# First batch of a fused attention and feed-forward kernel: K and Q loaded as fp32 half sequences and turned by TensorE, with one ordered queue behind them

## The chip, the cores and the metric

One core of a Trainium2 chip runs the kernel. It has TensorE for matmuls (PE in the rows; PEld is its weight load), VectorE (DVE), ScalarE (ACT), GpSimd (POOL) and SyncE (SP). DMAs are started from SP, ACT or POOL. The metric is device microseconds of one execution; lower is better.

## The reference

Attention with two kinds of heads, then a maxout feed-forward network over the concatenated heads. Shapes: B=4, H=8, S=768, D=64; 3072 tokens, d_model 512, d_ff 768; everything arrives as fp32.

```python
scores = scale * np.matmul(q, k.transpose(0, 1, 3, 2))
stream_keep = causal & (is_sink | in_win)      # 4 sinks, window 64
mask = where(is_retrieval head, causal, stream_keep)
scores = np.where(mask, scores, -1e9)
a = softmax(scores); attn = np.matmul(a, v)
x = attn.transpose(0, 2, 1, 3).reshape(B * S, H * D)
h = np.maximum(np.maximum(x @ w1, x @ w2), x @ w3)
out = h @ w_out
```

## The kernel before

The work goes by batch `b`, half sequence (384 queries) and quad of heads (`qd`, heads 0 to 3 or 4 to 7). `t` numbers these: t=0,1 are batch 0, half 0; t=2,3 batch 0, half 1; t=4,5 batch 1, half 0, and so on. `UNITS` splits each `t` into score units `u`: two for half 0, four for half 1. `SLOTS` lists all (t, u), and the main loop goes through the slots `n`: n=4 to 7 is t=2, n=8 to 11 is t=3, n=12 and 13 is t=4, n=14 is the first unit of t=5. What comes ahead of n=4 (t=0 and t=1) is written out by hand. The schedule is manual: each engine runs its instructions in the order of the program, and waits on semaphores.

A quad goes through these steps, with the line numbers of the profile:

- `load` (L114): K and Q by DMA from POOL, cast to fp16 on the way, one head in 32 partitions, into `kq`. Half sequences in batch 0 (L127), whole ones later (L120).
- `turn` (L137, L146): DVE transposes 32x32 blocks of `kq` into `KQ`, with the head dimension in two halves `r` of 32.
- `scores` (L346): on PE, four heads side by side in row groups of 32, two matmuls (`r`) for each piece, into `st`; for t<2 the mask is added by a matmul with the identity (`nm`, L378); ACT takes the exponential into `pt` (L384); for later `t` POOL multiplies the mask in (`masks`, `mk`, L407).
- `load_v`, `prep_v` (L153, L326): V by DMA as fp32, cast to `va` by DVE (L332); POOL makes `vf`, the copy for far blocks (L334).
- `av` (L411): `pt` times V on PE, then DVE divides into `x` (L431, L433).
- `turn_x` (L439): PE transposes `x`, DVE copies to `xT` (L452).
- `ffn` (L265): a generator of units, each 4 matmuls of 384 columns (L284) or 6 of 512 (L302, `woutt`); `fill(n)` runs n of them between the other work. The first feed-forward block takes all units of `w0t`, then `w1t`, then `w2t`, and needs one weight after the other.

In each slot the loop issues loads, `scores`, a waiting `turn_x`, about half of the paced feed-forward units, `av` of the previous `t`, `turn`s of the next batch, `prep_v`, and the rest of the units. `idle_work(8)` at the start is 8 matmuls on zeros. DMAs from one engine are issued in its program order, so POOL's order of `load`, `load_weight` and `masks` is also the order of its DMA queue.

Of the kernel before, what the change touches and what calls it, by code (L numbers as in the profile page):

```python
# [48 lines left out]
def kernel(  # L49
# [61 lines left out]
    staged = {}  # L111
    KQs = {}

    def load(b, qd, half=None):  # L114
        n = (HALF if half is not None else S) // R
        t0 = HALF if half == 1 else 0
        st = stage.tile([P, 2, S // R, D], FP16, tag="kq", name="kq")
        for i, src in enumerate((k, q)):
            if half is None:
                nc.gpsimd.dma_start(  # L120
                    out=st[:, i],
                    in_=src[b, G * qd : G * qd + G].rearrange(
                        "h (p j) d -> (h p) j d", p=R
                    ),
                )
            else:
                nc.gpsimd.dma_start(  # L127
                    out=st[:, i, 0:n],
                    in_=src[b, G * qd : G * qd + G, t0 : t0 + HALF].rearrange(
                        "h (p j) d -> h p j d", p=R  # L130
                    ),
                )
# [4 lines left out]
    def turn(b, qd, half, i, part=None):  # L137
        if (b, qd) not in KQs:
            KQs[b, qd] = qkt.tile([P, 2, S, 2], FP16, tag="KQ", name="KQ")
        st = staged[b, qd, half]  # L140
        n = (HALF if half is not None else S) // R
        t0 = HALF if half == 1 else 0
        j0, j1 = (0, n) if part is None else (part * n // 2, (part + 1) * n // 2)
        dst = KQs[b, qd][:, i, t0 : t0 + R * n].rearrange("c t two -> c (t two)").bitcast(FP32)
        srcap = st[:, i, j0:j1].rearrange("c j d -> c (j d)").bitcast(FP32)
# [200 lines left out]
    def scores(t, u):  # L346
        b, half, qd = where(t)
        early = t < NQ
        KQ = KQs[b, qd]
# [7 lines left out]
        m = G // len(sts)
        for ki, q0, n, c0 in UNITS[half][u]:
            t0 = half * HALF + q0 * P
            for r in range(2):  # L360
                for g in range(G):
                    rows = slice(R * g, R * g + R)
                    nc.tensor.matmul(  # L363
                        sts[g // m][:, g % m, c0 : c0 + n * P],
                        KQ[rows, 0, ki * P : (ki + 1) * P, r],
                        KQ[rows, 1, t0 : t0 + n * P, r],
                        start=(c0 == 0 and r == 0), stop=(r == 1 and not early),
                        skip_group_check=True, tile_position=(R * g, 0),
                    )
# [122 lines left out]
    load_weight(2)  # L492
    turn_x(1, 1)
    for i in range(2):
        turn(0, 0, 1, i)
    for hp in range(NHP):
        head_masks(hp, False)
    fill(4)

    FIRST = 4  # L500
    PLAN = {
    }
    loads = {}
    for b in range(1, B):
        o = (b - 1) * 12
        loads[o + (7 if b == 1 else 3)] = [lambda b=b: load(b, 0)]
        loads[o + (9 if b == 1 else 5)] = [lambda b=b: load(b, 1)]
# [81 lines left out]
```

## Time and profile before

| | |
|---|---|
| median of 3 runs | 222.61 us (221.78 to 223.77) |
| the profiled execution | 222.25 us |
| its span in the trace | 220.3 us |
| PE busy | 194.1 us (88%) |
| DVE, ACT, POOL busy | 137.4, 117.9, 130.0 us |
| mean DMA rate | 102 GB/s |

The profiled execution is 0.36 us below the median, and 1.95 us of it lie outside the span. Times in the rows count from the start of the span. Busy shares are means over the whole span.

### The profile page before, as it was taken

What the parts mean: (1) busy time and instruction counts of PE and PEld (TensorE: products, weight loads), DVE (VectorE), ACT (ScalarE), POOL (GpSimd) and SP (SyncE); (2) the same over time, 40 slices, a digit from 0 to 9 for tenths busy, and PEclk for the clock granted to TensorE, in tenths of its full rate; (3) what the DMA queues carried; (4) which work ended last, traced back from release to release, by engine and by line L of the source; (5) the groups of instructions that cost most, each with busy time, mean ns of one, the idle gap of its engine ahead of it and who ended that gap; (6) DMA issues with size and microseconds to landing.
All of it is one profiled execution on the core that took longest, in us unless ns stands there. A gap on an engine that the chain in (4) does not pass through costs nothing.

```text
span 220.3 us, 5254 instructions
## 1 busy us (share of the span) xinstructions
PE 194.1 (88%) x2160; PEld 110.7 (50%) x2160; DVE 137.4 (62%) x283; ACT 117.9 (54%) x174; POOL 130.0 (59%) x154
## 2 busy tenths in 40 slices
PE   6038699897569999999999999999999999999993
PEld 1024444452435654656556546555656456556651
DVE  2074877679748761896859654969495816564540
ACT  2009187566543568557375577566647675713222
POOL 7922007999969368357989482497892754730000
PEclk9758999999959999999999999999999999999999
DMA  4999996599803935910217819501200030003003
GB/s 100 166 184 188 200 204 111 100 197 196 226 3 53 167 70 137 268 29 0 98 49 136 152 62 280 93 0 41 106 3 0 3 144 3 0 3 143 0 3 144
DMA packets 34024, 22.38 MB, mean 102 GB/s; under 512 B 25872, under 2 KB 29200, under 8 KB 34000
## 3 DMA queue, kind: packets, MB, share of 16 engines
q0 software_dynamic: 8560, 10.24, 27.0%
q1 hardware_dynamic: 24256, 11.54, 21.1%
q10 hardware_dynamic: 1184, 0.27, 0.6%
q8 instruction: 17, 0.28, 0.5%
q14 instruction: 7, 0.06, 0.1%
HBM read 25.17 MB, written 6.29 MB: 143 GB/s over the span
## 4 chain that ended last, share of the span: by engine, by line
PE 61%; DVE 13%; POOL 8%; ACT 6%; DMA 5%; issue 5%; ACTq 0%; DVEq 0%; POOLq 0%
PE yy L284 29%; PE st L363 9%; PE yy L302 8%; PE oacc L423 8%; POOL pt L407 6%; DVE KQ L146 5%; DMA kq<-in_q_dram 5%; ACT pt L384 5%; PE yst L284 3%; DVE x L433 3%; PE tr L449 3%; DVE va L332 2%; DVE acc L295 2%; PE st L378 1%; PE yst L302 1%
## 5 line engine op out<-in xcount | busy, mean ns | idle before, releaser
L407 POOL TENSOR_TENSOR pt<-pt,mk 128x512 f16<-128x512 f16 x84 | 90.7, 1106 | 55.7 <-ACT pt L384 55.6
L384 ACT ACTIVATE pt<-st 128x1024 f16<-128x1024 f32 (+3 forms) x100 | 82.9, 888 | 39.4 <-PE st L363 25.1
L295 DVE TENSOR_TENSOR acc<-yy,acc 128x384 f16<-128x384 f32 x45 | 24.8, 553 | 40.0 <-ACT acc L292 29.6
L363 PE MATMUL st<-KQ 32*128 32x384 f16 (+2 forms) x640 | 30.3, 288 | 16.3 <-DVE KQ L146 14.7
L292 ACT CAST acc<-yy 128x384 f16<-128x384 f32 x45 | 21.6, 483 | 32.6 <-PE yy L284 28.1
L284 PE MATMUL yy<-xT,w0t 128*128 128x384 f16 x180 | 37.1, 331 | 0.0
L284 PE MATMUL yy<-xT,w1t 128*128 128x384 f16 x180 | 36.8, 331 | 0.0
L284 PE MATMUL yy<-xT,w2t 128*128 128x384 f16 x180 | 36.4, 326 | 0.0
L146 DVE STREAM_TRANSPOSE KQ<-kq 128x384 f32<-128x384 f32 x32 | 31.5, 1068 | 6.7 <-DMA kq<-in_k_dram 6.5
L363 PEld LDWEIGHTS <-KQ 32*128 32x128 f16 x640 | 13.3, 95 | 38.3 <-issue 17.6
L302 PE MATMUL yy<-woutt,hT 128*128 128x512 f16 x132 | 31.5, 379 | 0.0
L423 PEld LDWEIGHTS <-pt 128*128 128x128 f16 x672 | 24.9, 97 | 7.9 <-issue 3.1
L295 DVE TENSOR_TENSOR hT<-yy,acc 128x384 f16<-128x384 f32 x45 | 24.9, 554 | 3.9 <-PE yy L284 1.7
L423 PE MATMUL oacc<-va,pt 128*128 128x65 f16 x352 | 25.0, 193 | 2.2 <-ACT pt L384 1.1
L284 PEld LDWEIGHTS <-w1t 128*128 128x128 f16 x192 | 18.0, 99 | 12.0 <-issue 1.6
L284 PEld LDWEIGHTS <-w0t 128*128 128x128 f16 x192 | 17.7, 99 | 11.5 <-issue 1.5
L309 ACT COPY ot<-yy 128x512 f32<-128x512 f32 x22 | 12.9, 589 | 19.4 <-PE yy L302 16.6
L332 DVE CAST va<-vs 128x384 f16<-128x384 f32 x32 | 22.8, 724 | 0.0
L284 PEld LDWEIGHTS <-w2t 128*128 128x128 f16 x192 | 17.6, 97 | 10.1
L423 PE MATMUL oacc<-vf,pt 128*128 128x65 f16 x320 | 21.3, 193 | 0.7 <-DVE hT L295 0.7
L302 PEld LDWEIGHTS <-hT 128*128 128x128 f16 x144 | 13.2, 98 | 14.7 <-issue 1.3
L433 DVE TENSOR_TENSOR x<-oacc,rc 128x384 f16<-128x384 f32 x32 | 17.8, 557 | 1.1
(51 smaller groups left out, 111.4 us busy)
## 6 DMA issues: line engine op xcount, KB each, us to landing
out_dram<-ot SPq DMA_DIRECT2D x24, 256.0 KB, 2.1
vs<-in_v_dram SPq DMA_DIRECT2D x20, 256.0 KB, 5.2
kq<-in_k_dram POOLq DMA_DIRECT2D x6, 384.0 KB, 5.6
kq<-in_q_dram POOLq DMA_DIRECT2D x6, 384.0 KB, 7.0
kq<-in_k_dram POOLq DMA_DIRECT2D x4, 192.0 KB, 12.7
kq<-in_q_dram POOLq DMA_DIRECT2D x4, 192.0 KB, 13.5
w0t<-in_moe_w_dram POOLq DMA_DIRECT2D x1, 768.0 KB, 13.7
w1t<-in_moe_w_dram POOLq DMA_DIRECT2D x1, 768.0 KB, 18.6
```

The costliest lines, as they stand in the source:

```text
L146: nc.vector.transpose(out=dst.rearrange("c (p j) -> c j p", j=n)[:, j0:j1], in_=srcap.rearrange("c (j i) -> c j i", i=R),)
L284: nc.tensor.matmul(yy[:, 0:HALF], w_t[wi][:, ks, ni * P : (ni + 1) * P], xT[b, half][ks], start=(ks == 0), stop=(ks == KS - 1),)
L292: nc.scalar.copy(out=acc[ni], in_=yy[:, 0:HALF])
L295: nc.vector.tensor_tensor(out=dst, in0=yy[:, 0:HALF], in1=acc[ni], op=ALU.max)
L302: nc.tensor.matmul(yo[:, 0:DMdl], hT[ns][:, tb * P : (tb + 1) * P], woutt[:, ns, :], start=(ns == 0), stop=(ns == NNB - 1),)
L309: nc.scalar.copy(out=ot, in_=yo[:, 0:DMdl])
L332: nc.vector.tensor_copy(out=vdst, in_=vs[:, hs])
L363: nc.tensor.matmul(sts[g // m][:, g % m, c0 : c0 + n * P], KQ[rows, 0, ki * P : (ki + 1) * P, r], KQ[rows, 1, t0 : t0 + n * P, r], start=( ...
L384: nc.scalar.activation(out=pts[t, i][:, u, h0 : h0 + m, 0:w], in_=st[:, :, 0:w], func=AF.Exp, scale=sc,)
L407: nc.gpsimd.tensor_tensor(out=x, in0=x, in1=m, op=ALU.mult)
L423: nc.tensor.matmul(o[:, qi, hl, 0 : D + 1], pt[:, u, hl, c : c + P], vv[:, 2 * hp + hl, ki, 0 : D + 1], start=(idx == 0), stop=(idx == len ...
L433: nc.vector.tensor_tensor(out=x, in0=o[:, :, :, 0:D], in1=rc.unsqueeze(3).to_broadcast([P, HB, 2, D]), op=ALU.mult,)
```

## The change

It touches batch 0, and the places of some steps in the loop.

- K and Q of batch 0 are loaded as fp32, without a cast, in half sequences: 3 tokens (768 bytes) for each of 128 partitions and head. For half 0 the K loads go out on SP and the Q loads on ACT, as pair 0, pair 1, pairs 2 and 3 (a pair is two heads), ahead of V, which is now whole on SP.
- A `cast_pair` makes `kn` and `qn` in fp16 on DVE, ACT or POOL; `turn_pair` transposes the six blocks of a pair on PE and copies them out on DVE. `scores` of batch 0 then takes two heads side by side, 64 rows each, pair by pair.
- POOL issues, in this order: w0, K and Q of half 1 for pairs 0 and 1, w1, K and Q for pairs 2 and 3, w2, V of half 1, w_out, K and Q of batch 1. The V of batch 1 moves from POOL to SP, behind a two-element DMA that waits for an exponential of slot 8.
- The V cast of t=0 moves to POOL. In batch 0 `prep_v` of t=2 moves from slots 6 and 7 to 8 and 9 and `av` of t=2 from 8 and 9 to 9 and 10; in slots 12 and 13 the `turn`s of batch 1 now stand ahead of `av` of t=3. For later batches `prep_v` of the third `t` stands earlier in its slot, and the second quad's `turn`s one slot earlier.
- `idle_work` has 12 matmuls; the early masks share the tile `mk` with the later ones.

```diff
+    def load_pairs(half, hp, n, engines):
+        for nm, src, eng in zip(("ks", "qs"), (k, q), engines):
+            st = stage.tile([P, 4, HB, D], FP32, tag=nm, name=nm)
+            eng.dma_start(
+                out=st[:, 0 : 2 * n],
+                in_=src[
+                    0, 2 * hp : 2 * hp + 2 * n, half * HALF : (half + 1) * HALF
+                ].rearrange("h (p j) d -> p h j d", p=P),
+            )
+            for i in range(n):
+                staged.setdefault((half, hp + i), []).append(st[:, 2 * i : 2 * i + 2])
...
+    def cast_pair(half, hp, engines):
+        cast[half, hp] = []
+        for nm, src, op in zip(("kn", "qn"), staged.pop((half, hp)), engines):
+            x = half16.tile([P, HB, 2, D], FP16, tag=nm, name=nm)
+            op(out=x, in_=src.rearrange("p h j d -> p j h d"))
+            cast[half, hp].append(x)
...
+        tr = bank([P, 1024], FP16, "tr")
+        xs = cast.pop((half, hp))
+        for part in parts:
+            for i in part:
+                for j in range(HB):
+                    c = i * HALF + j * P
+                    nc.tensor.transpose(
+                        tr[:, c : c + P], xs[i][:, j].rearrange("p h d -> p (h d)"), ident
...
+            i0, i1 = part[0], part[-1] + 1
+            op(
+                out=of_pair(hp)[:, i0:i1, half * HALF : (half + 1) * HALF].rearrange(
+                    "p i (t j) -> p i t j", j=HB
+                ),
+                in_=tr[:, i0 * HALF : i1 * HALF].rearrange(
+                    "p (i j t) -> p i t j", i=i1 - i0, j=HB
...
+    after = consts.tile([1, 2], FP16, name="after")
+    def sync_after(x):
+        nc.sync.dma_start(out=after, in_=x)
...
-    load(0, 0, 0)
...
-    load_v(0, 0, (nc.sync, nc.scalar, nc.sync))
+    load_pairs(0, 0, 1, (nc.sync, nc.scalar))
+    load_pairs(0, 1, 1, (nc.sync, nc.scalar))
+    load_pairs(0, 2, 2, (nc.sync, nc.scalar))
+    load_v(0, 0)
...
-    load(0, 1, 0)
...
+        todo = [(i, part) for i in (pairs if b == 0 else (0,)) for part in UNITS[half][u]]
...
+                    if b == 0:
+                        KQ, rows = of_pair(2 * qd + i), slice(D * (g % 2), D * (g % 2) + D)
+                    else:
+                        KQ, rows = KQs[b, qd][:, :, :, r], slice(R * g, R * g + R)
...
-    idle_work(8)
+    dve, act, pool = nc.vector.tensor_copy, nc.scalar.copy, nc.gpsimd.tensor_copy
+    idle_work(12)
     head_flags()
-    turn(0, 0, 0, 0)
-    head_masks(0, True)
-    turn(0, 0, 0, 1)
-    head_masks(1, True)
-    scores(0, 0)
+    cast_pair(0, 0, (dve, act))
+    for hp in range(2):
+        head_masks(hp, True)
+    turn_pair(0, 0, dve)
+    cast_pair(0, 1, (pool, act))
+    turn_pair(0, 1, dve)
+    scores(0, 0, (0,))
+    cast_pair(0, 2, (dve, pool))
+    cast_pair(0, 3, (pool, pool))
+    load_weight(0)
+    head_masks(2, True)
+    scores(0, 0, (1,))
+    turn_pair(0, 2, dve)
+    scores(0, 1, (0,))
+    turn_pair(0, 3, dve)
+    head_masks(3, True)
+    scores(1, 0, (0,))
+    scores(0, 1, (1,))
+    scores(1, 0, (1,))
     for i in range(2):
-        turn(0, 1, 0, i)
-    for hp in range(2, NHP):
-        head_masks(hp, True)
-    scores(0, 1)
-    for i in range(2):
-        prep_v(0, i)
-    load_weight(0)
-    scores(1, 0)
-    load_v(0, 1)
-    load(0, 0, 1)
-    scores(1, 1)
+        prep_v(0, i, pool)
+    load_pairs(1, 0, 2, (nc.gpsimd, nc.gpsimd))
+    scores(1, 1, (0,))
     av(0, 0)
     av(0, 1)
+    scores(1, 1, (1,))
     for i in range(2):
-        prep_v(1, i)
+        prep_v(1, i, dve)
     load_weight(1)
-    load(0, 1, 1)
+    load_pairs(1, 2, 2, (nc.gpsimd, nc.gpsimd))
     turn_x(0, 0)
     turn_x(0, 1)
     av(1, 0)
     av(1, 1)
     turn_x(1, 0)
     load_weight(2)
+    load_v(0, 1, (nc.gpsimd,) * HB)
+    load_weight(3)
     turn_x(1, 1)
+    for hp in range(2):
+        cast_pair(1, hp, (dve, act))
+    fill(2)
+    for hp in range(2):
+        turn_pair(1, hp, dve)
+    for hp in range(NHP):
...
+            late = 1 if b == 0 else 0
+            put(o + (8 if late else 6) + i, late, prep_v, 4 * b + 2, i)
+            put(o + 10 + i, 2, prep_v, 4 * b + 3, i)
+            put(o + 8 + late + i, 1, av, 4 * b + 2, i)
+            put(o + 9 + late + i, "x", turn_x, 4 * b + 2, i)
...
+        if b + 1 < B:
+            put(o + (5 if b == 0 else 3), 0, load, b + 1, 0)
+            put(o + (8 if b == 0 else 5), 0, load, b + 1, 1)
+            if b == 0:
+                put(9, 0, lambda: sync_after(pts[3, 1][0:1, 0, 0, 0:2]))
+            put(o + (9 if b == 0 else 7), 0, load_v, b + 1, 0)
+            put(o + 11, 0, load_v, b + 1, 1)
+            for qd in range(2):
+                for x in range(2):
+                    for p in range(2):
+                        put(o + (10 if b == 0 else 8) + 2 * qd + x, 1, turn, b + 1, qd, x, p)
...
+        put(5, 1, cast_pair, 1, 2 + i, (dve, act))
+        put(6 + i, 1, turn_pair, 1, 2 + i, dve)
...
+        do(0)
+        if n < len(SLOTS):
+            scores(*SLOTS[n])
+        do("x")
```

On POOL, from its constants to the first weight; `w0t` is the first weight, `ks`/`qs` the fp32 loads, `kn`/`qn` their casts. Before:

```order
L127 DMA kq_117<-in_k_dram 128x1x768
L127 DMA kq_117<-in_q_dram 128x1x768
L235 COPY vf0_122<-far_128 128x32
L235 COPY vf1_123<-far_128 128x32
L334 TENSOR_TENSOR vf0_122<-vs_95,far_128 128x2x64 x2
L253 DMA w0t_131<-in_moe_w1_dram 128x4x768
L127 DMA kq_253<-in_k_dram 128x1x768
L127 DMA kq_253<-in_q_dram 128x1x768
```

After:

```order
L278 COPY vf0_132<-far_138 128x32
L278 COPY vf1_133<-far_138 128x32
L132 CAST kn_180<-ks_100 128x384
L132 CAST qn_205<-qs_106 128x384
L132 CAST kn_207<-ks_104 128x384
L132 CAST qn_209<-qs_106 128x384
L295 DMA w0t_140<-in_moe_w1_dram 128x4x768
L374 CAST va0_130<-vs_108 128x2x3x64
```

The issue of the first weight now stands behind four casts, the last of which needs the last load of half 0.

On POOL again, the queue behind it, up to the first load of batch 1 (`kq_503`). After:

```order
L119 DMA ks_286<-in_k_dram 128x4x192
L119 DMA qs_288<-in_q_dram 128x4x192
L376 TENSOR_TENSOR vf0_132<-vs_108,far_138 128x2x64 x2
L295 DMA w1t_141<-in_moe_w2_dram 128x4x768
L119 DMA ks_341<-in_k_dram 128x4x192
L119 DMA qs_343<-in_q_dram 128x4x192
L295 DMA w2t_142<-in_moe_w3_dram 128x4x768
L201 DMA vs_399<-in_v_dram 128x8x64 x3
L300 DMA woutt_143<-in_moe_w_out_dram 128x6x512
L167 DMA kq_503<-in_k_dram 128x1536
L167 DMA kq_503<-in_q_dram 128x1536
L455 TENSOR_TENSOR pt_475<-pt_475,mk_139 128x4x128
```

V of half 1 is in this queue now, ahead of `woutt`, and the first load of batch 1 stands ahead of the first mask.

On DVE in slots 11 to 13; `KQ_872` and `KQ_857` are the second quad of batch 1. Before:

```order
L332 CAST va0_120<-vs_249 128x2x3x64
L431 RECIPROCAL rc_868<-oacc_837 128x6
L433 TENSOR_TENSOR x_870<-oacc_837,rc_868 128x384
L146 STREAM_TRANSPOSE KQ_872<-kq_640 128x12x32 x2
L332 CAST va1_121<-vs_567 128x2x3x64
L452 COPY xT2_667<-tr_891 128x384
L431 RECIPROCAL rc_927<-oacc_896 128x6
L433 TENSOR_TENSOR x_929<-oacc_896,rc_927 128x384
L146 STREAM_TRANSPOSE KQ_872<-kq_640 128x12x32 x2
```

After:

```order
L374 CAST va0_130<-vs_399 128x2x3x64
L183 STREAM_TRANSPOSE KQ_857<-kq_610 128x12x32 x2
L479 RECIPROCAL rc_891<-oacc_860 128x6
L481 TENSOR_TENSOR x_893<-oacc_860,rc_891 128x384
L374 CAST va1_131<-vs_642 128x2x3x64
L500 COPY xT2_731<-tr_911 128x384
L183 STREAM_TRANSPOSE KQ_857<-kq_610 128x12x32 x2
L479 RECIPROCAL rc_949<-oacc_918 128x6
L481 TENSOR_TENSOR x_951<-oacc_918,rc_949 128x384
```

Each transpose of K or Q (`x2` is its two parts) now stands ahead of the division of its slot.

## Rows read from the trace of the kernel before

**Rows 1.** The page: DMA share in 40 slices of 5.5 us, in tenths.

```profile
DMA  4999996599803935910217819501200030003003
```

**Rows 2.** Stretches of 4 us: busy time of each engine, granted PE clock, DMA.

```profile
60.00:64.00 4.00, 1.55 (x20) 0.89 (x21) 2.80 (x5) 0.42 (x1) 3.01 (x4) 0.50 0.03 9
...
72.00:76.00 4.00, 4.00 (x63) 2.44 (x51) 3.10 (x8) 2.31 (x3) 1.61 (x4) 1.00 0.92 163
```

**Rows 3.** The chain that ended last: start, duration, what.

```profile
2.18 11.52 DMA kq<-in_q_dram
...
63.92 2.56 PE yy L284 x8
...
66.89 1.30 PE yy L284 x8
```

**Rows 4.** Timeline of PE: start, duration, count, idle time before and releaser.

```profile
14.63 1.04 PE L363 MATMUL st<-KQ 32*128 32x384 f16 x16 [9.77 <-DVE KQ L146]
...
26.66 2.88 PE L284 MATMUL yy<-xT,w0t 128*128 128x384 f16 x16
29.47 0.64 PE L363 MATMUL st<-KQ 32*128 32x384 f16 x16
...
39.22 0.89 PE L363 MATMUL st<-KQ 32*128 32x384 f16 x16
...
43.58 0.63 PE L363 MATMUL st<-KQ 32*128 32x384 f16 x16
...
47.31 0.64 PE L363 MATMUL st<-KQ 32*128 32x384 f16 x16
...
62.45 1.04 PE L363 MATMUL st<-KQ 32*128 32x384 f16 x16 [3.73 <-DVE KQ L146]
```

**Rows 5.** Timeline of DVE, 26 to 62 us.

```profile
48.53 2.07 DVE L146 STREAM_TRANSPOSE KQ<-kq 128x384 f32<-128x384 f32 x2
...
56.10 0.20 DVE L431 RECIPROCAL rc<-oacc 128x6 f32<-128x6 f32 x1 [1.53 <-PE oacc L423]
56.33 0.56 DVE L433 TENSOR_TENSOR x<-oacc,rc 128x384 f16<-128x384 f32 x1
```

**Rows 6.** Timeline of POOL.

```profile
6.99 0.85 POOL L253 DMA_DIRECT2D w0t<-in_moe_w_dram  x1
...
33.87 2.26 POOL L407 TENSOR_TENSOR pt<-pt,mk 128x512 f16<-128x512 f16 x2 [16.00 <-ACT pt L384]
...
38.81 0.82 POOL L334 TENSOR_TENSOR vf<-va,far 128x384 f16<-128x384 f16 x1
39.58 0.62 POOL L120 DMA_DIRECT2D kq<-in_k_dram  x1
```

**Rows 7.** Stretches of 1 or 2 us, columns as in rows 2 (the last is GB/s).

```profile
32.00:34.00 2.00, 1.87 (x22) 1.05 (x21) 0.38 (x1) 2.00 (x5) 0.13 (x1) 1.00 1.20 204
...
41.00:42.00 1.00, 0.02 (x1) 0.03 (x2) 0.46 (x1) 1.00 (x2) 1.00 (x2) 1.00 0.88 135
...
47.00:48.00 1.00, 1.00 (x22) 0.45 (x19) 0.92 (x2) 0.02 (x1) 1.00 (x3) 1.00 0.86 229
```

**Rows 8.** The DMAs of 3 to 3.5 us, then of 4 to 5.5 us.

```profile
DMA packets 222, 0.05 MB, mean 101 GB/s; under 512 B 222, under 2 KB 222, under 8 KB 222
...
DMA packets 1538, 0.38 MB, mean 256 GB/s; under 512 B 1538, under 2 KB 1538, under 8 KB 1538
```

**Rows 9.** DMA issues of 0 to 1 and 40 to 41 us: size, us to landing.

```profile
vs<-in_v_dram SPq DMA_DIRECT2D x1, 256.0 KB, 5.0
...
kq<-in_q_dram POOLq DMA_DIRECT2D x1, 384.0 KB, 6.2
```

**Rows 10.** Groups by line and form: count, busy time, mean ns of one, idle before.

```profile
L146 DVE STREAM_TRANSPOSE KQ<-kq 128x384 f32<-128x384 f32 x32 | 31.5, 1068 | 6.7 <-DMA kq<-in_k_dram 6.5
...
L292 ACT CAST acc<-yy 128x384 f16<-128x384 f32 x45 | 21.6, 483 | 32.6 <-PE yy L284 28.1 <-DVE hT L295 4.4
...
L452 DVE COPY xT<-tr 128x384 f16<-128x384 f16 x32 | 11.1, 350 | 6.6 <-PE tr L449 6.5
```

More of the change, by code (lines that the diff above doesn't have):

```diff
@@ L111 @@
     staged = {}
+    cast = {}
     KQs = {}
-    def load(b, qd, half=None):
-        n = (HALF if half is not None else S) // R
-        t0 = HALF if half == 1 else 0
+    def load_pairs(half, hp, n, engines):
[9 more added lines that the diff above has]
+                staged.setdefault((half, hp + i), []).append(st[:, 2 * i : 2 * i + 2])
@@ L117, in load @@
+    def load(b, qd):
         st = stage.tile([P, 2, S // R, D], FP16, tag="kq", name="kq")
         for i, src in enumerate((k, q)):
[L119 to L132, printed above, removed]
@@ L133, in load, with turn @@
-        staged[b, qd, half] = st
-    def turn(b, qd, half, i, part=None):
+            nc.gpsimd.dma_start(
+                out=st[:, i],
+                in_=src[b, G * qd : G * qd + G].rearrange("h (p j) d -> (h p) j d", p=R),
+            )
+        staged[b, qd] = st
+    def turn(b, qd, i, part):
         if (b, qd) not in KQs:
             KQs[b, qd] = qkt.tile([P, 2, S, 2], FP16, tag="KQ", name="KQ")
[L140 to L145, printed above, removed]
+        st = staged[b, qd]
+        n = S // R
+        j0, j1 = part * n // 2, (part + 1) * n // 2
+        dst = KQs[b, qd][:, i].rearrange("c t two -> c (t two)").bitcast(FP32)
+        src = st[:, i, j0:j1].rearrange("c j d -> c (j d)").bitcast(FP32)
@@ L323, in fill, with prep_v @@
                 queue.pop(0)
-    def prep_v(t, i):
+    def prep_v(t, i, op=None):
         b, half, qd = where(t)
@@ L363, in scores @@
                     nc.tensor.matmul(
                         sts[g // m][:, g % m, c0 : c0 + n * P],
[L365 to L368, printed above, removed]
+                        KQ[rows, 0, ki * P : (ki + 1) * P],
+                        KQ[rows, 1, t0 : t0 + n * P],
+                        start=(c0 == 0 and r == 0),
@@ L369, in scores @@
+                        stop=((b == 0 or r == 1) and not early),
+                        skip_group_check=True, tile_position=(rows.start, 0),
                     )
         w = max(c0 + n * P for _, _, n, c0 in UNITS[half][u])
-        for x, st in enumerate(sts):
+        for x, st in sts.items():
             i, h0 = m * x // 2, m * x % 2
@@ L492 @@
     load_weight(2)
+    load_v(0, 1, (nc.gpsimd,) * HB)
+    load_weight(3)
     turn_x(1, 1)
-    for i in range(2):
[L495 to L507, printed above, removed]
-        loads.setdefault(o + (8 if b == 1 else 7), []).append(lambda b=b: load_v(b, 0, (nc.gpsimd,) * HB if b == 1 else None))
-        loads.setdefault(o + 11, []).append(lambda b=b: load_v(b, 1))
@@ L527, with do @@
     for n in range(FIRST, len(SLOTS) + 3):
-        live = n < len(SLOTS)
-        t, u = SLOTS[n] if live else (NT4, n - len(SLOTS))
-        for f in loads.get(n, ()):
-            f()
-        if live:
-            scores(t, u)
-        if ready:
-            turn_x(*ready.pop(0))
+        def do(place):
+            for f in work.pop((n, place), ()):
+                f()
+        do(0)
+        if n < len(SLOTS):
+            scores(*SLOTS[n])
+        do("x")
         due += pace(n)
@@ L539 @@
         due -= part
-        if u < 2 and t > NQ:
-            av(t - 1, u)
-            ready.append((t - 1, u))
-        for f in turns.get(n, ()):
-            f()
-        x = u + 2 - len(UNITS[where(t)[1]]) if live else -1
-        if x >= 0:
-            prep_v(t, x)
+        do(1)
         part = int(due)
@@ L550 @@
         due -= part
-        if n == FIRST:
-            load_weight(3)
+        do(2)
+    assert not work
     while queue:
```

79 lines of the change are left out of this document (49 added, 30 removed).

## The prediction

> **What bounds the kernel now.** I read the busy slices first, then the chain of waits, then the timelines of PE, DVE and POOL around each wait of PE, then the DMA rows for what these waits end on. Three stages show. Until 14.63 us PE has no work of its own: the chain is one load of Q, 11.52 us long, and a transpose on DVE [rows 3, 4]. From 14.63 to 62.45 us PE is held up in turn by ACT, POOL and DVE; the last wait, 3.73 us at slot 14, is for a transpose of K and Q on DVE [rows 4]. From there PE has no gap worth counting (4.00 us busy of 4.00 in a late stretch, [rows 2]), and slot 14 is the first unit whose feed-forward work, that of batch 0 half 1, keeps it filled. So I take everything behind slot 14 as fixed and ask one thing: when does slot 14 begin? Each microsecond there is one at the end. The profiled 222.25 us are 62.45 to slot 14, 157.85 of span behind it and 1.95 outside the span; the median of three runs is 0.36 higher.
>
> The DMA engines are at nine tenths from the second slice to the sixth, and near that again from the ninth to the eleventh [rows 1], so an earlier start asks the same bytes of them earlier. That is the second thing to follow.
>
> **The change, part by part.**
>
> *Loads of half 0.* K and Q are 1.57 MB as fp32. At the 256 GB/s that two hardware queues moved in pieces of 256 bytes, against 101 GB/s in the half microsecond in which nearly all came from one [rows 8], they take 6.1 us from about 3 us on, the time of the first of these rows. A landing comes about 1.4 us behind the last data: the Q load issued behind K at 40.20 us lands after 6.2 us, at 46.4 [rows 6, 9], and the two, 768 KB written at 204 GB/s [rows 7], end 3.9 us after 41.1, where the 0.88 of a microsecond begins [rows 7]. So pair 0 lands near 6 us (a V load of 256 KB took 5.0 us from its issue, [rows 9]) and pairs 2 and 3 near 10.5.
>
> *Casts, transposes, copies.* A cast of 128x384 is at least the 0.48 us of ACT [rows 10] and at most, on POOL, the 0.82 us of a two-input operation of that size [rows 6]; I take 0.6. The Trainium skill (GPSIMD Engine Reference, Engine selection) calls one-input work on GpSimd roughly line-rate; no row here shows such a cast, and by that rule the two casts ahead of w0 would save 0.2 us together, which I leave out. A copy of a turned pair moves 768 elements to a strided place: 0.70 us as two copies of 384, 1.07 as a block transpose of the same bytes [rows 10]; I take 0.95. Eight copies replace eight block transposes, so DVE gains nothing and loses little.
>
> *First scores.* Pair 0 at 6.0, cast 0.5, four masks, copy 0.95: about 8.6 us, against 14.63. From there to the first feed-forward unit it was 12.0 us (26.66, [rows 4]); the same work gives 20.6. Two units follow, 1.3 us [rows 3], then the transposes of half 1: PE is ready for slot 4 near 22.9 us.
>
> *The queue on POOL.* Its cost is that w0 now waits for the last casts: 10.5 plus 0.6 gives 11.1 us against 6.99 [rows 6]. First data 1.5 us behind the issue (39.58 to 41.1, [rows 6, 7]): 12.6. A weight is 768 KB written, 3.9 us at 204 GB/s. Half of K and Q of half 1 is 0.79 MB, 3.4 us at the 229 GB/s of a stretch with V on POOL's queue [rows 7]; the nearest faster row gives 3.1. So w0 is through at 16.5, K and Q at 19.9, landed 21.3; two casts on ACT 22.3, transposes and copy 23.6. This and PE's own 22.9 plus the last copy meet: **slot 4 at 23.8 us**, 5.7 earlier than 29.47 [rows 4].
>
> *Slots 4 to 10.* They took 17.84 us (29.47 to 47.31). ACT gets two more casts, 0.96. Slots with `av` took 4.36 and 3.73, the four ahead 2.44 on average [rows 4]; one of the two moves behind slot 10: minus 1.3 to 1.9, I take 1.6. Twelve more transposes of 128 columns, and heads two instead of four side by side, are PE work in slots that ACT paces: if the two did not run together, a unit of 0.64 us would be some 0.6 longer, and 0.64 plus two units of feed-forward is 1.9 of 2.44, so 0 to 1 us over all, taken as 0. POOL was idle for 16.00 us ahead of its first mask [rows 6], which hides its new DMA issues and their waits. Slot 10 at 41.0.
>
> *Slots 10 to 14.* The first transpose of batch 1 began 1.22 us behind slot 10 [rows 4, 5]; the division of `av`, 0.20 and 0.56 [rows 5], now lies between: 43.0. Is K there? Behind 19.9 come w1, K and Q, w2, V, w_out: 3.9, 3.4, 3.9, 3.4, 3.9 is 38.4; K of batch 1 takes 1.9 and lands at 41.7, or up to 1.9 later where V of batch 1, now on SP, takes half the engines. Q follows 1.9 to 3.4 later and is wanted near 46.7. With loads at their slow ends the waits come to 3 us, at the fast ends to none; I take 1.4. From that transpose to slot 14 it was 13.92 us (48.53 to 62.45). In this DVE was idle 1.53 us for the result of `av` in slot 12 [rows 5], and the division of slot 13 (0.76) stood ahead of the last transpose; each division now stands behind the transpose of its slot. 11.6 us remain: **slot 14 at 56.0**, 6.4 us earlier.
>
> *Behind slot 14.* The moves in later batches fall where PE is full: nothing. The granted clock was 0.50, the 1.2 GHz level, from 60 to 64 us, where PE had little work and then a long wait [rows 2]; eight matmuls took 2.56 us there and 1.30 later [rows 3]. A shorter wait at slot 14 would give back some 1.8 us with the scores; since the wait stays, I count none.
>
> Sum: 222.25 minus 6.4 is 215.8, and with what I can't see, **216.0 us**.
>
> **The rivals.**
>
> *Slower: the 768-byte pieces move badly.* Everything hangs on how fast uncast loads go, and no row has such a piece. For it: one queue gave 101 GB/s. Against: two gave 256, with smaller pieces [rows 8]. At 150 GB/s half 0 takes 10.5 us, w0 goes out at 15.5, half 1 takes 5.2 us a load, slot 4 comes at 30, K of batch 1 lands near 52 to 54, and slot 14 at 65.6: 225.5 us. Below about 170 GB/s the change turns to a loss.
>
> *Little gained: the ordered queue is late at one place after another.* V of half 1 lands at 36 by the sum above, and DVE wants it, in order, at slot 8, near 36; w_out likewise at slot 10. A tenth more in the loads makes DVE wait there, the feed-forward results are not taken from PE, and the transposes of batch 1 begin 3 to 5 us later. For it: the queue has no slack in my own sum. Against: it had about as many bytes before. 220 us.
>
> *More gained: the loads are never late.* No wait for batch 1, a wait at slot 14 short enough for the clock to stay up (1.8), the casts and loads at their low ends: 212.5 us. The Trainium skill (DMA: Bandwidth & Descriptors, Specifications) has pieces from 512 bytes on at line rate; 768 bytes would then be such pieces. Nothing in the trace shows that size; what it shows, 256 bytes at 256 GB/s, is already not slow, so the rule makes this case somewhat likelier.
>
> **How the numbers follow.** Forecast 0.50 (its own range 214 to 218), little gained 0.22, more gained 0.13, slower 0.12, and 0.03 for the change not doing what it says, a load or cast serialized in a way that leaves the time as it is. The range reaches from 212.8 to 221.5: it leaves out the slower case, half of the larger gain and a little besides. A measurement of this kernel tells about 1% (2.2 us) from no change. Faster by more: 0.50 and 0.13 and half of 0.22, 0.74. Within: the other half and 0.03, 0.14. Slower: 0.12.
>
> **What would show it.** In the changed profile: first scores near 8.6 us; w0 issued near 11; slot 4 near 23.8; POOL's casts near 0.6 us; slot 14 near 56, with DVE transposing right ahead of it and without the 1.53 us idle; the rest as long as before, 157.85 us. It is wrong if slot 4 comes at 27 or later (the loads), if DVE waits for V near slot 8 or for K of batch 1 beyond 2 us (the queue), or if the stretch behind slot 14 changes by more than a microsecond (then that part was not fixed).

## The result, and the profile after

The changed kernel takes **212.95 us** (median of 4 runs, 212.57 to 213.63); beside it on the same chip the kernel before took 222.37 (221.78 to 223.77). The ratio is 0.957, 95% interval 0.952 to 0.963: faster by 4.3%. I had predicted 216.0 with a range from 212.8 to 221.5. The direction holds and the size was 3 us short: the time lies 0.15 us inside the range, two of the four runs lie below it, and it is below the forecast's own 214 to 218 and nearest to the rival of the larger gain (212.5).

The profiled execution took 213.63 us, with a span of 211.6. The DMA slices of the page, against [rows 1]:

```profile
DMA  3979999997029568201249397002100120012003
```

The dip of the seventh and eighth slice is gone (a small one is in the third), and the full stretch is over with the tenth. PE's timeline, against [rows 4]: first scores, first feed-forward unit, slots 4, 8, 10, 12, 14.

```profile
8.06 0.39 PE L410 MATMUL st<-KQ 64*128 64x384 f16 x4
...
19.36 1.47 PE L326 MATMUL yy<-xT,w0t 128*128 128x384 f16 x8 [0.29 <-DMA w0t<-in_moe_w_dram]
...
24.04 0.61 PE L410 MATMUL st<-KQ 64*128 64x384 f16 x8
...
34.00 0.39 PE L410 MATMUL st<-KQ 64*128 64x384 f16 x4
...
40.00 0.61 PE L410 MATMUL st<-KQ 64*128 64x384 f16 x8
...
48.42 0.63 PE L410 MATMUL st<-KQ 32*128 32x384 f16 x16 [1.49 <-DVE KQ L183]
...
54.19 1.00 PE L410 MATMUL st<-KQ 32*128 32x384 f16 x16 [1.51 <-DVE rc L479]
```

The first scores come 6.6 us earlier, slot 4 5.4, slot 14 8.3, and the span is 8.7 shorter. The wait at slot 14 is 1.51 us, for DVE, where it was 3.73. DVE there, against [rows 5]:

```profile
43.16 0.20 DVE L479 RECIPROCAL rc<-oacc 128x6 f32<-128x6 f32 x1 [1.54 <-PE oacc L471]
...
43.86 2.08 DVE L183 STREAM_TRANSPOSE KQ<-kq 128x384 f32<-128x384 f32 x2
...
52.06 2.07 DVE L183 STREAM_TRANSPOSE KQ<-kq 128x384 f32<-128x384 f32 x2
```

The four transposes of batch 1 lie between 43.86 and 54.19; none waits for a DMA. What DVE waits for ahead of them, 1.54 us, is the second `av` of t=2, which the change moved from slot 9 to slot 10. POOL at the start, against [rows 6]: the first and the last of its four casts, and the issue of the first weight.

```profile
6.71 0.51 POOL L132 CAST kn<-ks 128x384 f16<-128x384 f32 x1 [1.02 <-DMA ks<-in_k_dram]
...
10.67 0.51 POOL L132 CAST qn<-qs 128x384 f16<-128x384 f32 x1
11.12 0.93 POOL L295 DMA_DIRECT2D w0t<-in_moe_w_dram  x1
```

The windows over the loads of half 0, and from 18 to 20 us, over the weights and half 1 (last column GB/s), against [rows 7, 8]:

```profile
4.50:6.00 1.50, 1.50 (x5) 0.53 (x4) 1.35 (x7) 0.17 (x1) 0.47 (x2) 1.00 1.03 326
6.00:7.50 1.50, 1.15 (x11) 0.65 (x9) 1.21 (x4) 0.62 (x2) 0.51 (x1) 1.00 1.08 347
...
18.00:20.00 2.00, 1.32 (x10) 0.75 (x11) 1.25 (x4) 0.00 (x0) 2.00 (x3) 1.00 1.06 335
```

Pieces of 768 bytes (all but a few of the packets in the first two windows) moved at 326 to 347 GB/s, where I had taken 256. The Trainium skill (DMA: Bandwidth & Descriptors, Specifications) has pieces from 512 bytes on at line rate; the trace agrees in so far as these moved faster than the 256-byte pieces of [rows 8], and what line rate is no run here shows. The window of 18 to 20 us is the fastest of its stretch: from 20 to 36 us, the rest of the ordered queue, it was 253 GB/s. The DMA issues (us to landing), against [rows 9]: a first K load, w0, and K of batch 1, issued at 25.17.

```profile
ks<-in_k_dram SPq DMA_DIRECT2D x2, 192.0 KB, 4.8
...
w0t<-in_moe_w_dram POOLq DMA_DIRECT2D x1, 768.0 KB, 8.2
...
kq<-in_k_dram POOLq DMA_DIRECT2D x1, 384.0 KB, 13.2
```

So K of batch 1 is there at 38.4 us, 5.5 before its transpose. The groups (count, busy, mean ns), against [rows 10]:

```profile
L183 DVE STREAM_TRANSPOSE KQ<-kq 128x384 f32<-128x384 f32 x24 | 24.8, 1138 | 0.0
...
L153 DVE COPY KQ<-tr 128x768 f16<-128x768 f16 x8 | 7.5, 954 | 1.7 <-PE tr L149 1.7
...
L132 ACT CAST qn<-qs 128x384 f16<-128x384 f32 x6 | 2.9, 530 | 7.4 <-DMA qs<-in_q_dram 7.4
...
L132 POOL CAST qn<-qs 128x384 f16<-128x384 f32 x2 | 1.2, 576 | 2.3 <-DMA qs<-in_q_dram 2.3
```

The copy of a turned pair takes 0.954 us (0.95 in the sum). The 1.07 us of [rows 10], beside which I had set it, is a mean over all batches: the eight block transposes of batch 0, which these copies replace, took 0.83 to 0.85, so DVE loses 0.1 us on each. A cast of Q on POOL takes 0.576 (0.6) where ACT takes 0.530: the near line rate that the Trainium skill (GPSIMD Engine Reference, Engine selection) gives for one input agrees. The chain, against [rows 3]:

```profile
14.71 6.50 DMA qs<-in_q_dram
...
52.14 1.99 DVE KQ L183 x2
...
55.62 2.39 PE yy L326 x8
58.38 1.30 PE yy L326 x8
```

It holds the Q load of half 1, DVE's last transpose ahead of slot 14, and eight matmuls at 2.39 us that take 1.30 later: part of that stretch still ran at the lower granted clock, as in the kernel before (in the windows 1.00 is the 2.4 GHz level and 0.50 the 1.2 GHz level; a value between is a mixture).

### One table for every run

Since everything hangs on where slot 14 begins, I read four places from PE's timeline in each profiled run. Slot 15 is the second score unit of t=5.

| run | first scores | slot 4 | slot 4 to 14 | slot 14 to 15 | behind 15 | median us | ratio, 95% |
|---|---|---|---|---|---|---|---|
| before | 14.63 | 29.47 | 32.98 | 5.67 | 152.2 | 222.37 | |
| changed | 8.06 | 24.04 | 30.15 | 5.42 | 152.0 | 212.95 | 0.957 (0.952 to 0.963) |
| e12, changed again | 8.54 | 24.17 | 30.16 | 4.35 | 152.3 | 213.75 | 0.962 (0.954 to 0.970) |
| e1 | 15.18 | 31.70 | 34.11 | 4.27 | 152.3 | 224.37 | 1.005 (1.001 to 1.009) |
| e2 | 7.51 | 23.46 | 32.39 | 5.20 | 152.1 | 215.70 | 0.968 (0.964 to 0.973) |
| e3 | 8.80 | 26.40 | 30.16 | 4.32 | 152.3 | 212.83 | 0.957 (0.952 to 0.963) |
| e4 | 11.60 | 27.62 | 30.16 | 5.31 | 152.4 | 217.29 | 0.974 (0.970 to 0.978) |
| e5 | 12.94 | 30.58 | 30.17 | 4.32 | 152.3 | 218.99 | 0.980 (0.976 to 0.984) |
| e6 | 8.64 | 25.12 | 30.17 | 4.32 | 152.4 | 214.53 | 0.962 (0.958 to 0.966) |
| e7 | 7.74 | 23.54 | 30.16 | 5.98 | 151.9 | 213.39 | 0.958 (0.954 to 0.962) |
| e8 | 7.66 | 23.60 | 31.70 | 5.91 | 152.4 | 215.53 | 0.967 (0.962 to 0.972) |
| e9 | 8.88 | 24.43 | 29.03 | 4.38 | 152.6 | 212.45 | 0.956 (0.949 to 0.963) |
| e10 | 8.87 | 24.77 | 29.25 | 5.14 | 152.0 | 212.75 | 0.955 (0.950 to 0.961) |
| e11 | 8.71 | 24.38 | 29.21 | 6.45 | 152.3 | 213.38 | 0.958 (0.951 to 0.965) |

The ratios are against runs of the kernel before on the same chip (medians 223.53 us for e1, e2, e3 and e7, 223.04 for e4, e5, e6 and e8, 222.27 for e9 to e12). The changed kernel itself ran beside the kernel before and beside e9 to e12, not on the chips of e1 to e8; for those the stretches of the trace carry the readings more than a difference of medians. The time behind slot 15 is the same within 0.7 us in all of them. Slot 4 to 14 goes by the order of work: seven runs that leave that order as it is give 30.15 to 30.17, whatever happened ahead. Slot 14 to 15 is 4.3 to 4.4 us at the full clock and up to 6.5 below it. The 8.7 us of the change are 5.43 at slot 4, 2.83 between 4 and 14, 0.25 and 0.2 behind.

### The profile page after: what moved, and what is told of

Its sections match the earlier page's. It is cut to its first block, busy times and chain, and to the rows that moved or that the text cites. A ratio compares the mean times of both kernels' runs of the same rounds, so it can differ in the third digit from the quotient of the medians.

```text
span 211.6 us, 5225 instructions
## 1 busy us (share of the span) xinstructions
PE 197.5 (93%) x2132; PEld 112.6 (53%) x2132; DVE 136.5 (65%) x287; ACT 120.5 (57%) x178; POOL 130.0 (61%) x156
## 3 DMA queue, kind: packets, MB, share of 16 engines
HBM read 25.17 MB, written 6.29 MB: 149 GB/s over the span
## 4 chain that ended last, share of the span: by engine, by line
PE 74%; DMA 8%; DVE 8%; ACT 4%; issue 2%; POOL 1%; ACTq 0%; DVEq 0%
PE yy L326 37%; PE yy L344 12%; PE st L410 10%; PE oacc L471 8%; DVE KQ L183 4%; PE tr L497 3%; DMA qs<-in_q_dram 3%; ACT pt L432 3%; DMA vs<-in_v_dram 3%; PE yst L326 3%; DMA ks<-in_k_dram 2%; PE yst L344 1%; DVE acc L337 1%; DVE x L481 1%; ACT acc L334 1%
## 5 line engine op out<-in xcount | busy, mean ns | idle before, releaser
L455 POOL TENSOR_TENSOR pt<-pt,mk 128x512 f16<-128x512 f16 x84 | 90.6, 1104 | 35.3 <-ACT pt L432 32.2
L410 PE MATMUL st<-KQ 32*128 32x384 f16 (+5 forms) x560 | 29.3, 282 | 5.0 <-DVE rc L479 1.5
L410 PEld LDWEIGHTS <-KQ 32*128 32x128 f16 (+1 forms) x560 | 12.3, 93 | 24.5 <-issue 15.1
L183 DVE STREAM_TRANSPOSE KQ<-kq 128x384 f32<-128x384 f32 x24 | 24.8, 1138 | 0.0
L471 PE MATMUL oacc<-vf,pt 128*128 128x65 f16 x320 | 21.2, 193 | 0.7 <-DVE hT L337 0.7
L376 POOL TENSOR_TENSOR vf<-va,far 128x384 f16<-128x384 f16 x16 | 13.2, 826 | 11.8 <-DVE va L374 11.8
```

Source lines behind the costliest of these rows:

```text
L183: nc.vector.transpose(out=dst.rearrange("c (p j) -> c j p", j=n)[:, j0:j1], in_=src.rearrange("c (j i) -> c j i", i=R),)
L376: nc.gpsimd.tensor_tensor(out=vf[j][:, hs, k0:k1, 0:D], in0=vs[:, hs, 0:1] if half == 0 else va[j][:, hs, k0:k1, 0:D], in1=far[:, hs, k0:k ...
L410: nc.tensor.matmul(sts[g // m][:, g % m, c0 : c0 + n * P], KQ[rows, 0, ki * P : (ki + 1) * P], KQ[rows, 1, t0 : t0 + n * P], start=(c0 == ...
L455: nc.gpsimd.tensor_tensor(out=x, in0=x, in1=m, op=ALU.mult)
L471: nc.tensor.matmul(o[:, qi, hl, 0 : D + 1], pt[:, u, hl, c : c + P], vv[:, 2 * hp + hl, ki, 0 : D + 1], start=(idx == 0), stop=(idx == len ...
```

## The experiments

**The parts of the start (e4, e5, e6).** e4 issues half 0 from POOL, e5 loads V ahead of K, e6 issues w0 behind POOL's first cast.

```diff
# e4
-    load_pairs(0, 0, 1, (nc.sync, nc.scalar))
+    load_pairs(0, 0, 1, (nc.gpsimd, nc.gpsimd))
...
# e5
+    load_v(0, 0)
     load_pairs(0, 0, 1, (nc.sync, nc.scalar))
...
-    load_v(0, 0)
# e6
     cast_pair(0, 1, (pool, act))
+    load_weight(0)
...
-    load_weight(0)
```

> The changed kernel with the six fp32 loads of half 0 issued from POOL in place of SP and ACT. Theory A (the earlier start, of which the two hardware queues are a part): POOL spends 6 times 0.75 us on issues and its casts and w0 come later; pairs 2 and 3 land 2 us later or more, slot 4 at 26 or later, 215 to 217 us. Rival D (what counts is that nothing is queued ahead of K and Q and that they are not cast; the queue is indifferent): slot 4 within 0.7 of 24.0, 213 to 213.7.

> The changed kernel with V of half 0 ahead of K on SP, as V was ahead before. Theory A: V takes SP some 6.9 us to issue, so K of pair 0 lands 5 us later or more, w0 goes out later by as much, slot 4 at 28 or later: 217 to 219 us, half of the gain gone. Rival D2 (V and K share the engines anyway, and slot 4 ends on w0 and the loads of half 1): less than 1.5 us lost.

> The changed kernel with w0 issued on POOL behind its first cast, ahead of the three that need pairs 2 and 3. Theory A: w0 then lands before 17, K and Q of half 1 follow 1 to 2 us earlier than 20.3 and 21.3, slot 4 at 22.5 to 23.5: 211.5 to 212.7 us. Rival E (w0 takes the engines from pairs 2 and 3 and from V, half 0 ends later by what w0 wins): 212.7 to 214.

e4 took 217.29 us and e5 218.99, some 4 and 6 lost: e4 just above theory A's range, e5 inside it, with slot 4 at 27.62 and 30.58. In e4 it is not mainly the bytes: from 4 to 9 us they moved at 358 to 365 GB/s, and K of pair 0 landed at 6.5 us (5.0 in the changed kernel), but its cast on DVE began at 8.80. Timeline of POOL, then of DVE:

```profile
1.34 0.89 POOL L119 DMA_DIRECT2D ks<-in_k_dram  x1 [0.83 <-POOLq L641]
...
5.16 0.75 POOL L119 DMA_DIRECT2D qs<-in_q_dram  x1
```

```profile
7.20 0.29 DVE L245 TENSOR_TENSOR kept<-kept,base 128x256 f16<-128x256 f16 x1 [5.99 <-POOL kept L239]
```

Six issues hold POOL from 1.34 to 5.90, and the mask constants that it makes come behind them; DVE waits 5.99 us for one. The Trainium skill (DMA: Bandwidth & Descriptors, Rules for kernel authors) says that spreading DMAs over engines does not help bandwidth and saves only time of issue; here that is 0.72 to 0.89 us an issue, of an engine with other work. In e5, DVE's first cast, and SP's issues of K:

```profile
9.68 0.55 DVE L132 CAST kn<-ks 128x384 f16<-128x384 f32 x1 [4.30 <-DMA ks<-in_k_dram]
```

```profile
2.92 3.21 SPq L119 DMA_DIRECT2D ks<-in_k_dram  x3
```

The cast began at 5.07 in the changed kernel, so V's 0.79 MB ahead of K are 4.6 us. Some 2.1 of them are issue: SP issued K at 2.92, behind V, and at 0.81 in the changed kernel. The other 2.5 are the landing, 6.7 us for 4.2, beside V's bytes. w0 went out only 1.2 us later (12.33), where theory A had it as late as K.

The clock at the start differs too. PE waited 2.85 us (e4) and 4.38 (e5) for the first cast, and from 10 to 14 us the granted clock was 0.50 in both and 1.00 in the changed kernel. From the first scores to slot 4 the changed kernel took 15.98 us, e4 16.02 and e5 17.64, so up to 1.7 us of what e5 loses can be the clock and not V.

e6, 214.53 us, is above both expectations and shows no gain. POOL's timeline:

```profile
6.72 0.93 POOL L295 DMA_DIRECT2D w0t<-in_moe_w_dram  x1
...
15.63 0.51 POOL L374 CAST va<-vs 128x384 f16<-128x384 f32 x1 [4.50 <-issue]
```

w0 lands at 15.0 instead of 19.3, and V, loaded beside it, comes later: the cast of V begins at 15.63 instead of 12.1 (a V load took 10.5 us to land), `av` and the last unit of t=1 follow it, and the issue of half 1 stands behind it on POOL, at 17.25 instead of 13.89. The queue's order passed its delay from w0 to V. The first scores of this run were also at the lower clock (0.60 us for a unit of 0.39), so the whole 1.1 us at slot 4 can't be put on V.

**Idle matmuls (e3).**

```diff
-    idle_work(12)
+    idle_work(8)
```

> The changed kernel with 8 matmuls on zeros at the start, not 12. Theory A: PE waits for loads at slot 4 anyway, so 0 to 0.5 us lost, 213.0 to 213.5, even if the first scores run at a clock of 0.5. Rival C (the clock at the start is part of the gain: before, the first scores ran at 0.5): 1 to 2 us lost, 214 to 215.

212.83 us, the same by the median, as theory A had it. The profiled execution, at 215.24, came to slot 4 2.4 us later than the changed kernel: the stretch from 10 to 14 us had the clock at 0.50, the 1.2 GHz level, with PE idle ahead of it for 1.11 and 1.05 us of waits for casts; in the changed kernel it was 1.00.

```profile
10.00:14.00 4.00, 4.00 (x30) 2.30 (x28) 2.61 (x5) 2.71 (x4) 4.00 (x9) 0.50 0.52 83
```

Of its six runs four lie at 212.3 to 212.9 and two at 215.0 to 215.2, rival C's range, so what a low clock at the start costs is what rival C had. But eight matmuls are not shown to be worse than twelve: e10, with twelve, fell too (0.68 from 10 to 14 us), and e12, also with twelve, kept 1.00 behind a wait of 1.11 us.

**The loop (e1, e2, e7, e8).** e1 is the kernel before with the moves of the loop alone. e2 puts `av` of t=3 ahead of the transposes again, e7 undoes the moves in later batches, e8 issues the V of batch 1 from POOL in slot 9.

```diff
# e2
...
+        fs.insert(0 if f is av and n in (12, 13) else len(fs), lambda: f(*args))
...
# e7
...
+        fs.insert(0 if f is av and n > 13 else len(fs), lambda: f(*args))
...
-            put(o + (8 if late else 6) + i, late, prep_v, 4 * b + 2, i)
+            put(o + (8 if late else 6) + i, 1 if late else 2, prep_v, 4 * b + 2, i)
...
-                        put(o + (10 if b == 0 else 8) + 2 * qd + x, 1, turn, b + 1, qd, x, p)
+                        put(o + (10 + 2 * qd if b == 0 else 8 + 3 * qd) + x, 1, turn, b + 1, qd, x, p)
...
# e8
-            if b == 0:
-                put(9, 0, lambda: sync_after(pts[3, 1][0:1, 0, 0, 0:2]))
-            put(o + (9 if b == 0 else 7), 0, load_v, b + 1, 0)
+            put(o + (9 if b == 0 else 7), 0, load_v, b + 1, 0, (nc.gpsimd,) * HB if b == 0 else None)
```

> The kernel before with only the moves in the main loop (prep_v and av of t=2 two and one slots later, turns of batch 1 ahead of av of t=3, the moves in later batches); loads, casts and the start as before. Theory A (the gain is the earlier start of half 0, carried to slot 14 by the queue; the moves are worth the idle 1.53 us and one division of 0.76 at most): 220 to 222 us, slot 14 at 60 to 62. Rival B (the moves carry half of the gain or more, in slots 9 to 14 and in later batches): 218 or less.

> The changed kernel with av of t=3 put back ahead of the turns of batch 1 in slots 12 and 13. Theory A by my sum: DVE idles for av again and one division stands ahead of the last turn, slot 14 up to 2.3 us later, 214 to 215.3 us. Rival B: more than 2.3 us lost. Rival A2 (POOL is now ahead, so that av's result is there in time and the order no longer matters): under 0.8 us lost, 213.0 to 213.7.

> The changed kernel with the moves in batches 1 to 3 undone (prep_v of the third t at the end of its slot, the second quad's turns one slot later, av ahead of turns). Theory A: PE is full behind slot 14, so 0 to 0.5 us lost, 213.0 to 213.5. Rival B: 2 us or more lost, 215.

> The changed kernel with the first V of batch 1 issued from POOL at slot 9, without the small DMA on SP, as before the change. Theory A: 2.7 us of issues stand ahead of masks of t=3, DVE waits longer for av of t=2 and t=3, slot 14 is 0.5 to 2 us later: 213.5 to 215. Rival: POOL's idle 2.41 us in slots 10 to 11 takes the issues in, no difference.

e1 gained nothing, 224.37 us, against both expectations. Slot 4 to 14 is 1.13 us longer than before; DVE waits 3.36 us for `av` of t=2 (first row: DVE, of e1). Slot 14 to 15, at the full clock there, gives 1.4 us back. The first feed-forward units took 4.07 us for the 2.88 of [rows 4], which is the clock (0.67 in that stretch, 1.00 before; second row: PE).

```profile
49.72 0.20 DVE L431 RECIPROCAL rc<-oacc 128x6 f32<-128x6 f32 x1 [3.36 <-PE oacc L423]
```

```profile
27.70 4.07 PE L284 MATMUL yy<-xT,w0t 128*128 128x384 f16 x16
```

e2 lost 2.23 us between slots 4 and 14, for 2.3 in my sum (1.53 idle and 0.76 of division); its median, 215.70, is a little above theory A's range. DVE's timeline shows the idle time back again:

```profile
49.56 0.20 DVE L479 RECIPROCAL rc<-oacc 128x6 f32<-128x6 f32 x1 [1.59 <-PE oacc L471]
```

e8 lost 1.54 us there, and its median, 215.53, is above theory A's 215. POOL's timeline of it, then a V cast on DVE:

```profile
37.17 2.73 POOL L201 DMA_DIRECT2D vs<-in_v_dram  x3
39.91 2.40 POOL L455 TENSOR_TENSOR pt<-pt,mk 128x512 f16<-128x512 f16 x2
```

```profile
39.08 2.23 DVE L374 CAST va<-vs 128x384 f16<-128x384 f32 x1
```

Three issues hold POOL for 2.73 us in front of a mask that began at 37.94 in the changed kernel. The V cast beside them took 0.91 us there. e7, 213.39 us, is in theory A's range: undoing the later moves is not told apart from the changed kernel.

**What is left between slots 4 and 14 (e9 to e12).** e9 puts `prep_v` and `av` of t=2 back where they were. e10 puts the first two transposes of batch 1 ahead of `av` in slot 10; e11 does so and gives the V casts of slots 10 to 13 to ACT. e12 is the changed kernel beside them.

```diff
# e9
-            put(o + (8 if late else 6) + i, late, prep_v, 4 * b + 2, i)
+            put(o + 6 + i, 2 if late else 0, prep_v, 4 * b + 2, i)
-            put(o + 8 + late + i, 1, av, 4 * b + 2, i)
+            put(o + 8 + i, 1, av, 4 * b + 2, i)
...
# e10, e11
...
+        fs.insert(0 if f is turn and n == 10 else len(fs), lambda: f(*args))
# e11
-                put(o + i, 2, prep_v, 2 * NQ * b, i)
+                put(o + i, 2, prep_v, 2 * NQ * b, i, *((act,) if b == 1 else ()))
...
-            put(o + 10 + i, 2, prep_v, 4 * b + 3, i)
+            put(o + 10 + i, 2, prep_v, 4 * b + 3, i, *((act,) if b == 0 else ()))
```

> The changed kernel with prep_v of t=2 back in slots 6 and 7, and its av back in slots 8 and 9. By the terms of my sum (A) one av comes back ahead of slot 10 (1.6 us later there), and its division no longer stands ahead of the first transpose of batch 1, where DVE waited 1.54 us: 212.5 to 213.6 us, slot 10 near 41.5, slot 14 near 54.5. Rival (B): the move was needed because V of half 1 now lands at 31 us; DVE then waits for it near 28 to 31 us with the feed-forward maxima queued behind, and 2 to 3 us are lost: 215 to 216 us.

> The changed kernel with the first two transposes of batch 1 (slot 10) ahead of the av of that slot. K landed at 38.4 us in the changed kernel and its transpose began at 43.86, behind a wait of 1.54 us for av. If the chain of DVE from there sets slot 14 and batch 1's loads are not late (A), the transpose starts near 41.6, slot 14 comes 1.3 to 1.6 us earlier (near 52.7) and the time is 211.2 to 211.8 us. Rival (B): the loads or the later divisions hold the chain, and what is gained at slot 10 is waited for at slot 12 or 13: 212.5 to 213.3 us.

> As the run with the first transposes ahead of av, and also the V casts of slots 10 to 13 on ACT in place of DVE (0.41, 0.40 and 0.63 us of them lay in DVE's chain from 43.86 to slot 14). If DVE is what sets slot 14 (A), another 1.0 to 1.4 us: 210.0 to 210.8 us, slot 14 near 51.5. Rival (C): ACT's exponentials of these slots, or Q of batch 1 (landed 40.3 us), come last instead, and it is no faster than that run: 211.2 to 211.8 us.

> The changed kernel itself, unaltered, beside the other three on one chip: 212.6 to 213.4 us, slot 4 near 24 and slot 14 near 54 us, by every theory. What it measures is how far slot 14 and the span move between executions of one program.

e9, 212.45 us: slot 8 to 10 was 7.21 us against 6.00, so one `av` there is 1.2 us, but slot 14 came 1.13 earlier, counted from slot 4, than with the move; theory A had it later. DVE's casts of V of half 1, which landed at 31.3 to 32.8 us in the changed kernel, wait for nothing even in the earlier slots:

```profile
33.49 0.36 DVE L374 CAST va<-vs 128x384 f16<-128x384 f32 x1
...
35.56 0.58 DVE L374 CAST va<-vs 128x384 f16<-128x384 f32 x1
```

e10, 212.75 us, in its rival's range: 0.91 us less between slots 4 and 14, of 1.3 to 1.6 expected. The transpose did start earlier, at 42.27 with slot 4 at 24.77, which is 2.3 us nearer to slot 4. Of that 1.4 went again behind it: the division (0.73) now stands in that stretch, and a V cast took 1.04 us for 0.40 (DVE, then PE):

```profile
42.27 2.07 DVE L183 STREAM_TRANSPOSE KQ<-kq 128x384 f32<-128x384 f32 x2
```

```profile
54.02 1.04 PE L410 MATMUL st<-KQ 32*128 32x384 f16 x16 [1.51 <-DVE rc L479]
```

e11, 213.38 us: some 1.5 us of casts gone from DVE, and slot 14 no earlier than in e10. DVE, then PE:

```profile
51.19 0.36 DVE L500 COPY xT<-tr 128x384 f16<-128x384 f16 x1 [1.21 <-PE tr L497]
```

```profile
50.48 0.40 PE L410 MATMUL st<-KQ 32*128 32x256 f16 x6 [0.62 <-ACT pt L432]
```

DVE waits for transposes of `x` that stand on PE behind scores that wait for ACT: the rival of that run. The last transpose of batch 1 stands behind that copy in DVE's order.

None of the three is told apart from e12 by its time. The profiled runs say why: what was gained ahead of slot 14 was less than what the clock can take behind it. The window from 52 to 56 us (PE first, the granted clock third from the end) of the changed kernel, of e12 and of e11:

```profile
52.00:56.00 4.00, 2.49 (x43) 1.60 (x40) 3.93 (x7) 1.23 (x3) 4.00 (x6) 0.79 0.01 4
```

```profile
52.00:56.00 4.00, 2.27 (x49) 1.51 (x46) 3.95 (x7) 1.58 (x4) 4.00 (x6) 1.00 0.03 8
```

```profile
52.00:56.00 4.00, 2.50 (x26) 1.33 (x24) 2.46 (x5) 1.57 (x3) 4.00 (x6) 0.55 0.03 8
```

The first two are one program with one order, and PE waits 1.5 us ahead of slot 14 in both; in the one the clock fell, in the other not, and slot 14 to 15 took 5.42 and 4.35 us. e11 reached slot 14 first of the three (53.59) and slot 15 last (60.04).

## Why the prediction was right, and where its size was off

The mechanism held: half 0 comes in sooner, the ordered queue carries that to slot 4, DVE's transposes of batch 1 set slot 14, and what stands behind it hardly changes. The terms between slots 4 and 14 were off, and one wait that I had counted was not there.

The account on the profiled execution, predicted and found: slot 4 at 23.8 and 24.04; from slot 4 to 14 32.2 and 30.15; behind slot 14 157.85 and 157.41. Together 2.25 us less span than summed, 2.05 of it in the middle term. The median lies another 0.7 below the profiled run, and 0.2 I had added for what I couldn't see. That the last term fits so well is luck: both profiled executions, before and after, ran slot 14 to 15 at the lower clock. In e12 the clock stayed up and the stretch behind slot 14 took 156.67 us, 1.2 less than the 157.85 of the kernel before, more than the microsecond that I had named as the sign that this part is not fixed.

- **Half 0.** Landing near 6 and 10.5 us, casts, copies, w0 at 11.1: right (5.0 to 9.5, and 11.12). First scores came 0.5 earlier than summed. e4 and e5 show that both parts of this start, the two queues and K ahead of V, are needed; how much of e5's loss is the clock is not separated.
- **Slot 4.** Half 1 lands at 21.2 (14.71 and 6.50 in the chain), for 21.3 summed; slot 4 was 0.24 late. Right.
- **Slots 4 to 10.** Mis-sized: 15.96 us for 17.2. Slots 4 to 8 took 9.96, and 9.75 before, and 9.97 in e9, which has `prep_v` there as before: the 0.96 charged for two more casts on ACT came out as 0.2, all changes there together; 8 to 10 took 6.00 for 8.09 before, a gain of 2.1 where I took 1.6 for the moved `av`, of which e9 gives 1.2 to the move itself.
- **The wait for batch 1.** Mis-sized, and the step that failed: I had K land at 41.7 and counted 1.4 us. It landed at 38.4 and no transpose waited for it. w_out landed at 36.5, where the sum has 39.8, and K 1.9 behind it, as summed: the loads from 20 to 36 us ran at 253 GB/s, above the 204 to 229 that I had taken. In its place DVE waits 1.54 us for the `av` that was moved into slot 10. So the transpose stood 3.86 us behind slot 10, for 3.4 summed: near by luck, since it was another wait.
- **From that transpose to slot 14.** 10.33 us for 11.6. The 2.3 us of the reordered divisions were right (e2: 2.23). A further 1.3 I had not seen. They are the three V casts in this chain, 1.7 us shorter together than before, less one copy of `xT` that it now has more (0.3); the table below has them.
- **V of batch 1 on SP.** I had costed it as a delay of up to 1.9 us to K's landing. It is a gain of 1.54 us, since POOL no longer issues it (e8).
- **`prep_v` and `av` of t=2 later.** I had taken this as a gain of 1.6 us ahead of slot 10. It is one there (1.2 in e9), and a loss of 1.13 by slot 14 (e9).
- **What these three make together.** Each is what the changed kernel loses or wins when one piece is taken out of it, and they do not add up to an account of the gain: e1 has the reordered divisions and the later `av` with the old loads, by these terms 1.1 us won between slots 4 and 14, and it lost 1.13. Why it lost so much ahead of the transposes is not taken apart.
- **Behind slot 14.** Fixed to 0.4 us here, but not as I gave it: behind slot 15 it is fixed, and the score unit and the feed-forward between the two take 4.3 to 6.5 us by the clock.
- **The rivals.** Slower pieces are out (326 GB/s against a break-even of 170). The late queue is out: V of half 1 landed at 31.3 to 32.8, w_out at 36.5 (issued at 21.91, 14.6 us), both before they were wanted. The larger gain, 212.5, holds in one of its two parts, that no load of batch 1 is late; the other, that the clock stays up, held in e12 and not in the run profiled first.

Split at the first transpose of batch 1 on DVE, the stretch from slot 4 to slot 14 reads like this (us; the last column has the three V casts between that transpose and slot 14):

| run | slot 4 to that transpose | from it to slot 14 | V casts |
|---|---|---|---|
| before | 19.06 | 13.92 | 1.94, 0.44, 0.76 |
| e1 | 23.71 | 10.40 | 0.40, 0.40, 0.62 |
| changed | 19.82 | 10.33 | 0.41, 0.40, 0.63 |
| e2 | 19.83 | 12.56 | 0.40, 0.40, 0.71 |
| e8 | 21.37 | 10.33 | 0.40, 0.40, 0.62 |
| e9 | 18.37 | 10.66 | 0.96, 0.45, 0.59 |
| e10 | 17.50 | 11.75 | 0.35, 1.04, 0.55 |

All of the gain here, 3.6 us, lies behind that transpose, and the order of the loop brings it with the old loads too (e1); ahead of it the changed kernel loses 0.8. What makes a V cast short or long stands beside it on POOL. Before, the first of the three casts (DVE) and the masks beside it (POOL):

```profile
50.40 1.94 DVE L332 CAST va<-vs 128x384 f16<-128x384 f32 x1
```

```profile
47.56 4.55 POOL L407 TENSOR_TENSOR pt<-pt,mk 128x512 f16<-128x512 f16 x4
```

The masks end at 52.11 and the cast at 52.34. In both kernels every V cast on DVE of more than 0.45 us, 18 before and 16 after, ends 0.21 to 0.23 us behind the end of a two-input operation on POOL; those with none beside them take 0.35 to 0.41. So a new order also moves the length of these casts. No run changes that alone.

Open is what decides whether the clock falls at slot 14: the same program did both.
